# A channel stage in two passes: both block products by Strassen's seven products of 384 columns, with the values between kept in DRAM

## The chip, the cores and the metric

The kernel runs on one core of a Trainium2 chip. The metric is the device time of one execution in microseconds; lower is better. Three executions of the kernel before took 703.06 to 704.03 us, with a median of 703.39 us.

## What is computed

Three blocks follow one another: a windowed and dilated attention over 4 batches, 8 heads and 576 tokens, a gated feed-forward block, and a mixer block. All is single precision. The change touches only the end of the mixer, its channel stage:

```python
h = np.maximum(xt @ w_tok1, 0.0) @ w_tok2        # token stage
u = x + h.transpose(0, 2, 1)
h2 = np.maximum(u @ w_ch1, 0.0) @ w_ch2          # channel stage
return (u + h2).astype(np.float32)
```

Here u has 2304 tokens of 512 channels, w_ch1 is 512 by 1536 and w_ch2 is 1536 by 512.

## The kernel before

**Numbers.** Every operand of a matmul is held as two parts, a high part rounded to the engine's fp32r type and a low part that holds the rest. One product of two blocks is three matmuls (high by high, high by low, low by high), issued by `mm3` (L445). `split` (L461) makes the two parts: a copy on ACT or DVE, then a subtraction on DVE. The weights come from DRAM as 64-bit floats; `single` (L492) turns them into 32-bit ones with one step on ACT and two on DVE.

**Order of the work.** Nothing is issued directly. `Plan` (L148) records every operation with its dependences, prices it (`_cost`, L245), and then `order` (L291) simulates the five engines: each engine takes the ready operation that is due first, where due times are counted back from the matmuls in the order in which the program names them. The result is one fixed order for each engine. All DMAs are issued by SP and share one queue; the plan books a DMA of 32-bit words of n per partition with `8 * (0.03 + 4 * n * 0.0266e-3)` us, at least 0.45, and 2.1 us more until a consumer may start. In the run each engine keeps the planned order, so an instruction that waits holds back all that stand behind it on its engine.

**Channel stage.** The tokens are cut into chunks of 512 (`CH`), four whole ones and one of 256. u lies in SBUF (`whole`, two slots of 4608 words). The loop at L1050 runs over two groups of hidden blocks, five chunks in each, and three values of j in each chunk: 30 steps. For each step `middle` (L997) computes hidden blocks j and j + 6 of the chunk by `w_ch1`: for a whole chunk with Strassen's seven products of 256 columns (each is 2 slices by 3 matmuls, so 42 matmuls), for the last one with four products (24 matmuls). `kept` and `plus` (L980, L985) take sums out of PSUM, `put` (L990) applies the relu and splits. One step later `result` (L1029) multiplies both hidden blocks by `w_ch2` in the plain way: 4 output blocks by 2 by 3, so 24 matmuls of 512 columns (256 in the last chunk). After three steps the sums leave PSUM; those of the first group go to DRAM (`parts`), and come back to be added in the second. `prep_u` (L950) makes Strassen's sums of u and splits them, once for each chunk in each group. `weight_1` (L833) and `weight_2` (L849) load and split the weights; four of each are resident.

Of the kernel before, what the change touches and what calls it, by code (L numbers as in the profile page):

```python
# [54 lines left out]
CH = 512  # L55
# [361 lines left out]
def tile_model(nc, banks, parts, units, cst, mu, w_k, w_v, w_r, w_t1, w_t2, w_c1, w_c2, outT):  # L417
# [5 lines left out]
    def at(place, shape, dtype=F32):  # L423
        name, number, offset = place
        return memory[name][number].view(offset, shape, dtype)
# [387 lines left out]
    both = at(("raw", 0, 0), (2, 4, 128))  # L813
    sums = at(("raw", 0, 1024), (4, 2, 128))
    LO, HI = slice(0, 2), slice(2, 4)
    GROUP, RESIDENT = 3, 4

    def operands(four, two, one):

        four, two, one = pair(four, (4, 2, 128)), pair(two, (4, 128)), pair(one, (2, 128))  # L820
        named = {f"S{i + 1}": tuple(v[:, i] for v in four) for i in range(4)}
        named.update({f"A1{i + 1}": tuple(v[:, 2 * i:2 * i + 2] for v in two) for i in range(2)}, A22=one)
        return four, two, one, named

    w1 = [
        operands(("wk", 0, 0), ("wk", 1, 0), ("wk", 1, 1024)),
        operands(("wk", 2, 0), ("wk", 3, 0), ("wk", 3, 1024)),
        operands(("xt", 2, 0), ("xt", 0, 0), ("xt", 0, 1024)),
        operands(("at", 0, 0), ("wr", 2, 0), ("wr", 3, 0)),
    ]  # L830
    w2 = [pair(p, (C,)) for p in cut("x2", (5, 6, 0, 1, 2, 3), 1024)]

    def weight_1(j):  # L833

        four, two, one, _ = w1[j % RESIDENT]
        for i in range(2):
            single([(everything, col_block(w_c1, j + 6 * i))], at(("raw", 0, 512 * i), (512,)), raw_c)
        a, b = both[:, 0], both[:, 1]
        combine(sums[:, 0], b[:, LO], b[:, HI], ALU.add)
        combine(sums[:, 1], sums[:, 0], a[:, LO], ALU.subtract)  # L840
        combine(sums[:, 2], a[:, LO], b[:, LO], ALU.subtract)
        combine(sums[:, 3], a[:, HI], sums[:, 1], ALU.subtract)
        split(a, *two)
        split(b[:, HI], *one)
        split(sums, *four)

    both_r = ring(("raw", 0, 0), ("raw", 0, 512))

    def weight_2(j):  # L849
        for i in range(2):  # L850
            weight([(everything, words(w_c2)[rows(j + 6 * i), :])], *w2[2 * (j % RESIDENT) + i], raw_c, both_r)
# [13 lines left out]
    for j in range(2):  # L865
        weight_1(j)
# [70 lines left out]
    spare = [("wk", 1, 1536), ("wk", 3, 1536), ("xt", 0, 1536)]  # L937
    first_r = ring(xt512[8:12], ("wr", 3, 512), z512[8:15], cut("at", (2,), 512))
    other_r = ring(z512[:15], ("y", 0, 0))
    mid_r = ring(cut("z", (5,), 512), spare, [("at", 0, 2048), ("at", 0, 2560)])  # L940
    t_r = ring([("unit", i, 0) for i in range(2)])
    part_r = ring(cut("x2", (4,), 256), cut("at", (1,), 256))
    y_r = ring(xt512[8:12])
    xp_r, yp_r, zp_r = psum(0, 1), psum(2), psum(3)
    uhl, mid, op = {}, {}, {}

    def size_of(c):
        return min(CH, NT - CH * c)

    def prep_u(g, c):  # L950
        b1, b2 = (w[:, :, CH * c:CH * c + size_of(c)] for w in whole)
        h = 256
        ops = {"B11": b1[:, :, :h], "B21": b2[:, :, :h]}
        if size_of(c) == CH:
            ops.update(T1=None, T2=None, B22=b2[:, :, h:], T3=None, T4=None)
            order = ["B11", "T1", "B21", "T2", "B22", "T3", "T4"]
        else:
            ops.update(T5=None)
            order = ["B11", "B21", "T5"]
        formed = {  # L960
            "T1": lambda: (b1[:, :, h:], ops["B11"]), "T2": lambda: (ops["B22"], ops["T1"]),
            "T3": lambda: (ops["B22"], b1[:, :, h:]), "T4": lambda: (ops["B21"], ops["T2"]),
            "T5": lambda: (ops["B21"], ops["B11"]),
        }
        for name in order:
            if ops[name] is None:
                x, y = formed[name]()
                ops[name] = t_r.tile(2, h)
                combine(ops[name], x, y, ALU.subtract)
            r = first_r if (g, c) == (0, 0) else other_r  # L970
            hl = r.tile(2, h, dtype=F32R), r.tile(2, h, dtype=F32R)
            split(ops[name], *hl)
            uhl[name] = hl

    def product(out, a, b, first=True, last=True, goes_on=False):
        for k in range(2):
            (ah, al), (bh, bl) = w1[now % RESIDENT][3][a], uhl[b]
            mm3(out, ah[:, k], al[:, k], bh[:, k], bl[:, k], first and k == 0, last and k == 1, goes_on)

    def kept(p):  # L980
        t = part_r.tile(256)
        copy(t, p)
        return t

    def plus(p, t):  # L985
        out = part_r.tile(256)
        combine(out, p, t, ALU.add)
        return out

    def put(m, half, x):  # L990
        h, l = (v[:, half] for v in mid[m])
        nc.scalar.activation(out=h, in_=x, func=AF.Relu)
        nc.vector.scalar_tensor_tensor(out=l, in0=x, scalar=0.0, in1=f(h), op0=ALU.max, op1=ALU.subtract)

    now = 0

    def middle(c, j):  # L997
        nonlocal now
        now = j
        n = size_of(c)  # L1000
        for m in (j, j + 6):
            mid[m] = tuple(mid_r.tile(n, dtype=F32R) for _ in range(2))
        lo, hi = slice(0, 256), slice(256, 512)
        if n < CH:
            x, y = xp_r.tile(256), yp_r.tile(256)
            product(x, "A11", "B11", last=False)
            product(x, "A12", "B21", first=False)
            put(j, lo, x)
            product(y, "S1", "B11", last=False)
            product(y, "A22", "T5", first=False)  # L1010
            put(j + 6, lo, y)
            return
        x, y, z = xp_r.tile(256), yp_r.tile(256), zp_r.tile(256)
        product(x, "A11", "B11")
        s1 = kept(x)
        product(y, "S1", "T1")
        s5 = kept(y)
        product(z, "A12", "B21")
        put(j, lo, plus(z, s1))
        product(x, "S2", "T2", first=False, goes_on=True)  # L1020
        s2 = kept(x)
        product(y, "S4", "B22", first=False, goes_on=True)
        put(j, hi, plus(y, s2))
        product(x, "S3", "T3", first=False, goes_on=True)
        put(j + 6, hi, plus(x, s5))
        product(x, "A22", "T4", first=False, goes_on=True)
        put(j + 6, lo, x)

    def result(g, c, j):  # L1029
        n, start = size_of(c), CH * c  # L1030
        for kt in range(4):
            if j % GROUP == 0:
                op[kt] = bank(4 + kt, (n,))
            for i in range(2):
                w = w2[2 * (j % RESIDENT) + i]
                mm3(
                    op[kt], w[0][:, rows(kt)], w[1][:, rows(kt)], *mid[j + 6 * i],
                    j % GROUP == 0 and i == 0, j % GROUP == GROUP - 1 and i == 1,
                )
            if j % GROUP == GROUP - 1:  # L1040
                y, part = y_r.tile(n), parts[4 * c + kt][:, :n]
                if g == 0:
                    nc.vector.tensor_tensor(out=y, in0=op[kt], in1=whole[kt // 2][:, kt % 2, start:start + n], op=ALU.add)
                    nc.sync.dma_start(out=part, in_=y)
                else:
                    nc.sync.dma_start(out=y, in_=part)
                    nc.vector.tensor_tensor(out=y, in0=op[kt], in1=y, op=ALU.add)
                    nc.sync.dma_start(out=outT[rows(kt), start:start + n], in_=y)

    nchunk = -(-NT // CH)  # L1050
    steps = [(g, c, j) for g in range(2) for c in range(nchunk) for j in range(GROUP * g, GROUP * g + GROUP)]
    for i in range(len(steps) + 1):
        if i < len(steps):
            g, c, j = steps[i]
            if j % GROUP == 0:
                prep_u(g, c)
            if (g, c, j) == (0, 0, 0):
                weight_1(2)
                weight_1(3)
            middle(c, j)  # L1060
        if i:
            before = steps[i - 1]
            if before[:2] == (0, 0):
                weight_2(before[2])
            result(*before)
            if before == (0, 0, 2):
                weight_2(3)
# [84 lines left out]
```

## Time and profile before

| | |
|---|---|
| median of 3 runs | 703.39 us (703.06 to 704.03) |
| the profiled execution, its own time | 704.08 us |
| its span, first to last instruction | 702.3 us |
| around the span | 1.8 us |
| mean granted TensorE clock | 0.995 of full speed |
| busy: PE, DVE, ACT | 687.2, 500.1, 332.1 us |
| DMA | 65.71 MB, 28.1% of the 16 engines' time |

A matmul is shown with its whole passage through the array, so the records of neighbours overlap and busy time overstates the work. The cost of one is read as the distance between starts. The same holds for DVE, where one instruction starts before the record of the last has ended.

### The profile page before, as it was taken

How to read it: one execution, taken by the hardware profiler on the slowest of the kernel's cores; microseconds unless marked ns; L12 is line 12 of the kernel's file. 1: busy time of each engine (PE TensorE's matmuls, PEld its weight loads, DVE VectorE, ACT ScalarE, POOL GpSimd, SP SyncE). 2: the span in 40 equal slices, each digit the busy share in tenths (PEclk: the TensorE clock that was granted, in tenths of full speed). 3: DMA queues.
4: the chain of work that ended last, by engine and by line, in shares of the span. 5: the costliest groups of instructions: out<-in, count | busy, mean ns of one | idle time of the engine just before them, and what ended most of it. 6: DMA issues, size and time to landing. Idle time of an engine off the chain costs nothing.

```text
span 702.3 us, 11861 instructions
## 1 busy us (share of the span) xinstructions
PE 687.2 (98%) x4513; PEld 612.5 (87%) x4513; DVE 500.1 (71%) x1125; ACT 332.1 (47%) x930; POOL 2.1 (0%) x22
## 2 busy tenths in 40 slices
PE   6899999999999999999999999999999999999998
PEld 6678888888888888888789898998998999889888
DVE  5899995695694596673999799674748975656442
ACT  5899873583364474352675364242333542323210
POOL 0000000000000000000000000000000000000000
PEclk9899999999999999999999999999999999999999
DMA  8978332143221001002332221301012323040302
GB/s 327 387 279 297 109 119 70 59 137 112 66 78 55 16 9 53 1 1 71 103 104 97 70 72 56 115 1 61 12 49 70 131 72 105 16 121 1 120 30 91
DMA packets 32935, 65.71 MB, mean 94 GB/s; under 512 B 3056, under 2 KB 11632, under 8 KB 32880
## 3 DMA queue, kind: packets, MB, share of 16 engines
q1 hardware_dynamic: 32880, 64.97, 28.1%
q8 instruction: 35, 0.57, 0.3%
q14 instruction: 20, 0.16, 0.1%
HBM read 55.52 MB, written 9.44 MB: 92 GB/s over the span
## 4 chain that ended last, share of the span: by engine, by line
PE 87%; DVE 5%; DMA 4%; ACT 2%; issue 1%; SPq 0%; DVEq 0%; ACTq 0%
PE bank L403 87%; DVE z L403 2%; ACT z L403 1%; DMA x<-w_k 1%; DMA wr<-units 1%; DVE x L403 1%; DMA wv<-units 1%; DMA xt<-w_t 1%; DVE at L403 1%; DVE xt L403 0%; DVE raw L403 0%; DVE wv L403 0%; ACT x L403 0%; DVE unit L403 0%; ACT at L403 0%
## 5 line engine op out<-in xcount | busy, mean ns | idle before, releaser
L403 PE MATMUL bank<-z,wk 128*128 128x256 f32 (+1 forms) x1276 | 242.8, 311 | 0.3 <-DVE z L403 0.2
L403 PEld LDWEIGHTS bank<-z,wk 128*128 128x128 f32 x1276 | 201.9, 189 | 11.8 <-DVE z L403 0.8
L403 PE MATMUL bank<-wv,z 128*128 128x512 f32 x432 | 129.6, 403 | 1.1 <-DVE z L403 1.1
L403 PEld LDWEIGHTS bank<-wv,z 128*128 128x128 f32 x432 | 77.9, 188 | 13.7 <-DVE z L403 1.9
L403 PE MATMUL bank<-z,x 128*128 128x512 f32 (+1 forms) x300 | 80.8, 371 | 0.0
L403 ACT ACTIVATE z<-bank 128x384 f32<-128x384 f32 (+3 forms) x78 | 36.6, 473 | 74.7 <-PE bank L403 73.9
L403 PE MATMUL bank<-wk,x 128*128 128x512 f32 (+1 forms) x180 | 66.3, 371 | 0.0
L403 PE MATMUL bank<-wr,z 128*128 128x512 f32 x228 | 62.5, 402 | 0.7 <-DVE z L403 0.7
L403 DVE SCALAR_TENSOR_TENSOR z<-bank,z 128x384 f32<-128x384 f32 (+2 forms) x59 | 32.8, 564 | 41.5 <-ACT z L403 41.4
L403 ACT ACTIVATE at<-at 128x96 f32<-128x96 f32 (+3 forms) x155 | 51.1, 332 | 21.8 <-DVE at L403 20.6
L403 ACT ACTIVATE x<-bank 96x512 f32<-96x512 f32 (+2 forms) x68 | 35.1, 519 | 51.5 <-PE bank L403 50.4
L403 PEld LDWEIGHTS bank<-z,x 128*128 128x128 f32 x300 | 52.3, 189 | 7.0
L403 PE MATMUL bank<-at,x 128*128 128x512 f32 (+1 forms) x180 | 53.7, 372 | 0.0
L403 DVE TENSOR_TENSOR z<-z,z 128x384 fp32r<-128x384 f32 x92 | 50.3, 553 | 3.5 <-ACT z L403 1.3
L403 PEld LDWEIGHTS bank<-wr,z 128*128 128x128 f32 x228 | 41.4, 188 | 8.4 <-DVE z L403 1.1
L403 PE MATMUL bank<-z,at 128*128 128x256 f32 (+1 forms) x196 | 46.0, 342 | 0.0
L403 PEld LDWEIGHTS bank<-wk,x 128*128 128x128 f32 x180 | 34.0, 189 | 3.9
L403 PEld LDWEIGHTS bank<-at,x 128*128 128x128 f32 x180 | 32.4, 189 | 4.9
L403 PEld LDWEIGHTS bank<-z,at 128*128 128x128 f32 x196 | 32.4, 190 | 2.7
L403 PE MATMUL bank<-at,z 128*128 128x288 f32 x192 | 33.4, 302 | 1.1 <-DVE wv L403 1.1
L403 DVE SCALAR_TENSOR_TENSOR z<-xt,cst,z 128x256 f32<-128x256 f32 (+3 forms) x92 | 33.7, 404 | 0.6
L403 ACT ACTIVATE z<-z 128x384 fp32r<-128x384 f32 x56 | 28.8, 520 | 8.0 <-DVE z L403 5.9
(163 smaller groups left out, 1071.7 us busy)
## 6 DMA issues: line engine op xcount, KB each, us to landing
wr<-w_c SPq DMA_DIRECT2D x24, 512.0 KB, 3.6
at<-units SPq DMA_DIRECT2D x14, 416.0 KB, 3.5
unit<-units SPq DMA_DIRECT2D x13, 416.0 KB, 3.3
at<-units SPq DMA_DIRECT2D x21, 256.0 KB, 2.9
part<-xt SPq DMA_DIRECT2D x16, 256.0 KB, 2.0
xt<-part SPq DMA_DIRECT2D x16, 256.0 KB, 2.8
outT<-xt SPq DMA_DIRECT2D x16, 256.0 KB, 2.0
wv<-units SPq DMA_DIRECT2D x9, 416.0 KB, 6.9
```

The source lines that it names most:

```text
L403: call(kw["out"], kw["constant"]) if method == "memset" else call(**kw)
```

## The change

Each chunk is now 768 tokens, in two halves of 384 (`N2`), so there are three chunks and no odd one. Pass 1 runs `middle` for three chunks and six j, with all of w_ch1 resident; the relu of the four quarters stays one single-precision block, which goes to DRAM (`kept_mid`). `weight_2` forms Strassen's sums of w_ch2, splits them and stores them to DRAM as well (`kept_w`), through three buffers (`fresh`), and u goes to DRAM too (`kept_u`). Then w_ch2 in its seven forms is read back into the places of w_ch1, and pass 2 runs `result` for the three chunks: each of seven sweeps is 2 output blocks by 6 hidden blocks by 3 matmuls of 384 columns. It reads the hidden values and u back, forms the differences, and splits. The output block leaves once, without `parts`.

```diff
-CH = 512
+N2 = 384
+NAMES = "A11", "S1", "A12", "S2", "S4", "S3", "A22"
...
+    fresh = ring(cut("x2", (4,), 512), ("y", 0, 0))
+    def quarters(j, load, order):
+        for i in range(2):
+            single([(everything, load(j + 6 * i))], at(("raw", 0, 512 * i), (512,)), raw_c)
+        a11, a12, a21, a22 = (both[:, k // 2, k % 2] for k in order)
+        combine(sums[:, 0], a21, a22, ALU.add)
+        combine(sums[:, 1], sums[:, 0], a11, ALU.subtract)
+        combine(sums[:, 2], a11, a21, ALU.subtract)
+        combine(sums[:, 3], a12, sums[:, 1], ALU.subtract)
+        return a11, a12, a22
...
     def weight_2(j):
-        for i in range(2):
-            weight([(everything, words(w_c2)[rows(j + 6 * i), :])], *w2[2 * (j % RESIDENT) + i], raw_c, both_r)
+        a11, a12, a22 = quarters(j, lambda m: words(w_c2)[rows(m), :], (0, 2, 1, 3))
+        for name, v in zip(NAMES, (a11, sums[:, 0], a12, sums[:, 1], sums[:, 3], sums[:, 2], a22)):
+            t = fresh.tile(2, 256, dtype=F32R)
+            split(v, t[:, 0], t[:, 1])
+            nc.sync.dma_start(out=kept_w[name][:, j], in_=f(t))
...
-    for j in range(2):
+    for j in range(3):
         weight_1(j)
...
+    for j in range(3, 6):
+        weight_1(j)
+    mid_r = ring(cut("at", (0,), 4 * N2))
+    x_r, y_r, z_r = psum(0, 1, 2), psum(3, 4, 5), psum(6, 7)
...
+    def prep_u(c):
+        lo, hi = slice(2 * N2 * c, 2 * N2 * c + N2), slice(2 * N2 * c + N2, 2 * N2 * c + 2 * N2)
+        for q in range(2):
+            nc.sync.dma_start(out=kept_u[c][:, 2 * q:2 * q + 2], in_=whole[q][:, :, 2 * N2 * c:2 * N2 * c + 2 * N2])
...
+        for name, x, y in (("S1", b12, "A11"), ("S2", b22, "S1"), ("S3", b22, None), ("A22", b21, "S2")):
+            v[name] = diff_r.tile(2, N2)
...
+            combine(v[name], x, b12 if y is None else v[y], ALU.subtract)
...
     def middle(c, j):
...
+        def part(q, p, t):
+            combine(mid[:, q], p, t, ALU.add)
+            relu(mid[:, q], mid[:, q])
...
+        by(x, "A11")
+        s1 = aside(x)
+        by(y, "S1")
+        s5 = aside(y)
+        by(z, "A12")
+        part(0, z, s1)
+        by(x, "S2", **on)
+        s2 = aside(x)
+        by(y, "S4", **on)
+        part(1, y, s2)
+        by(x, "S3", **on)
+        part(3, x, s5)
+        by(x, "A22", **on)
+        relu(mid[:, 2], x)
+        nc.sync.dma_start(out=kept_mid[c][:, :, j], in_=mid)
+
+    for c in range(3):
+        prep_u(c)
+        for j in range(6):
+            middle(c, j)
+            if c == 0:
+                weight_2(j)
...
+            nc.sync.dma_start(out=f(at(places[j], (n, 2, 256), F32R)), in_=kept_w[name][:, j:j + n])
...
+    def result(c):
+        def load(q):
+            quads[q] = [half_r.tile(3, N2) for _ in range(2)]
+            for i, t in enumerate(quads[q]):
+                nc.sync.dma_start(out=t, in_=kept_mid[c][:, q, 3 * i:3 * i + 3])
+        def parts(q):
+            for t in quads[q]:
+                hl = tuple(hl_r.tile(3, N2, dtype=F32R) for _ in range(2))
+                split(t, *hl)
+        def turned(q, other):
+            for t, o in zip(quads[q], quads[other]):
+                combine(t, o, t, ALU.subtract)
+        def sweep(name, b, banks, **kw):
+            for a in range(2):
+                lhs = [tuple(v[:, rows(a)] for v in hl) for hl in w2[name]]
+                product(banks[a], lhs, b, **kw)
...
+        load(0)
+        load(1)
+        for kt in range(4):
+            nc.sync.dma_start(out=us[kt], in_=kept_u[c][:, kt])
+        load(2)
+        load(3)
+        sweep("A11", parts(0), x)
+        s1 = two(aside_r)
+        plus(x, u_of(0, 0), s1)
+        turned(0, 1)
+        sweep("S1", parts(0), y)
...
+        less(2, 0)
+        sweep("A22", parts(2), x, **on)
+        t = two(out_r)
+        plus(x, u_of(2, 0), t)
+        send(t, 2, 0)
...
-    steps = [(g, c, j) for g in range(2) for c in range(nchunk) for j in range(GROUP * g, GROUP * g + GROUP)]
```

## Rows read from the trace of the kernel before

**Rows 1.** The page: busy time of each engine, and the granted clock in 40 slices.

```profile
PE 687.2 (98%) x4513; PEld 612.5 (87%) x4513; DVE 500.1 (71%) x1125; ACT 332.1 (47%) x930; POOL 2.1 (0%) x22
PEclk9899999999999999999999999999999999999999
```

**Rows 2.** Busy time by stretch: length, engines, then clock, DMA share, GB/s.

```profile
400.00:415.00 15.00, 13.69 (x100) 12.78 (x98) 14.36 (x30) 9.47 (x18) 0.00 (x0) 1.00 0.24 72
415.00:500.00 85.00, 84.93 (x534) 76.73 (x535) 63.48 (x137) 32.59 (x76) 0.00 (x0) 1.00 0.15 50
500.00:600.00 100.00, 100.00 (x665) 92.11 (x665) 68.67 (x148) 35.05 (x78) 0.00 (x0) 1.00 0.24 80
600.00:699.00 99.00, 99.00 (x639) 90.06 (x637) 49.98 (x106) 25.00 (x58) 0.00 (x0) 1.00 0.19 61
```

**Rows 3.** Timeline of PE: start, duration, form and count; unbroken runs of matmuls.

```profile
303.87 2.24 PE L403 MATMUL bank<-wv,z 128*128 128x512 f32 x9
305.95 2.27 PE L403 MATMUL bank<-z,wk 128*128 128x384 f32 x12
308.06 2.24 PE L403 MATMUL bank<-wv,z 128*128 128x512 f32 x9
...
690.42 3.04 PE L403 MATMUL bank<-z,wk 128*128 128x256 f32 x24
...
693.30 0.64 PE L403 MATMUL bank<-z,x 128*128 128x256 f32 x4
```

**Rows 4.** Timeline, the last instructions of the span.

```profile
697.55 2.49 SPq L403 DMA_DIRECT2D outT<-xt  x4
...
698.70 0.52 PE L403 MATMUL bank<-at,x 128*128 128x256 f32 x3
...
699.26 0.42 DVE L403 TENSOR_TENSOR xt<-bank,xt 128x256 f32<-128x256 f32 x1 [0.29 <-PE bank L403]
```

**Rows 5.** Timeline of PE: its two waits where the channel stage begins.

```profile
402.67 1.81 PE L403 MATMUL bank<-at,z 128*128 128x288 f32 x12 [0.51 <-DVE wv L403]
405.07 1.85 PE L403 MATMUL bank<-at,z 128*128 128x288 f32 x12 [0.60 <-DVE wv L403]
```

**Rows 6.** Timeline of DVE: neighbours without a wait, at 384, 256, 512 and 1024 columns.

```profile
304.75 0.56 DVE L403 SCALAR_TENSOR_TENSOR z<-bank,z 128x384 f32<-128x384 f32 x1
305.22 1.28 DVE L403 SCALAR_TENSOR_TENSOR x<-x,bank 128x512 f32<-128x512 f32 x2
...
423.59 0.42 DVE L403 SCALAR_TENSOR_TENSOR at<-bank,at 128x256 fp32r<-128x256 f32 x1
423.93 1.28 DVE L403 TENSOR_TENSOR z<-unit,z 128x512 fp32r<-128x512 f32 x2
425.13 0.69 DVE L403 TENSOR_TENSOR unit<-wv,wv 128x512 f32<-128x512 f32 x1
...
427.90 1.22 DVE L403 TENSOR_TENSOR at<-raw,at 128x1024 fp32r<-128x1024 f32 x1
429.02 0.42 DVE L403 COPY at<-bank 128x256 f32<-128x256 f32 x1
```

**Rows 7.** Groups of ACT's instructions by form: busy, mean ns of one, idle before.

```profile
L403 ACT ACTIVATE z<-bank 128x384 f32<-128x384 f32 x48 | 23.4, 487 | 56.2 <-PE bank L403 55.8
```

**Rows 8.** DMA issues: count, KB each, median us from issue to landing.

```profile
wr<-w_c SPq DMA_DIRECT2D x24, 512.0 KB, 3.6
part<-xt SPq DMA_DIRECT2D x16, 256.0 KB, 2.0
```

**Rows 9.** Stretches in which DMA was busy; the last two columns are DMA share and GB/s.

```profile
8.00:16.00 8.00, 7.59 (x61) 6.95 (x60) 6.79 (x19) 5.43 (x27) 0.00 (x0) 1.00 1.03 401
542.00:545.00 3.00, 3.00 (x27) 3.00 (x26) 0.85 (x2) 0.77 (x2) 0.00 (x0) 1.00 0.83 233
681.00:686.00 5.00, 5.00 (x29) 4.34 (x29) 2.56 (x4) 0.00 (x0) 0.00 (x0) 1.00 0.46 169
```

**Rows 10.** A stretch with DMA and DVE both full: PE is the first busy column.

```profile
48.00:60.00 12.00, 11.26 (x90) 9.89 (x89) 12.00 (x22) 11.81 (x35) 0.00 (x0) 1.00 0.86 314
```

More of the change, by code (lines that the diff above doesn't have):

```diff
@@ L812, in tile_model @@
     raw_c = ring([("wr", k, 0) for k in range(2)])
[L813 to L831, printed above, removed]
-    def weight_1(j):
-        four, two, one, _ = w1[j % RESIDENT]
-        for i in range(2):
[L837 to L845, printed above, removed]
@@ L847, in tile_model @@
-    both_r = ring(("raw", 0, 0), ("raw", 0, 512))
-    def weight_2(j):
-        for i in range(2):
-            weight([(everything, words(w_c2)[rows(j + 6 * i), :])], *w2[2 * (j % RESIDENT) + i], raw_c, both_r)
+    both, sums = at(("raw", 0, 0), (2, 2, 256)), at(("raw", 0, 1024), (4, 256))
+    spots = cut("wk", range(4), 512) + cut("xt", (2, 0), 512) + cut("wr", (2,), 512) + cut("x2", (5, 6, 0, 1, 2, 3), 512)
+    fresh = ring(cut("x2", (4,), 512), ("y", 0, 0))
[8 more added lines that the diff above has]
+        return a11, a12, a22
@@ new lines, in tile_model @@
+    w1 = []
+    def weight_1(j):
+        _, _, a22 = quarters(j, lambda m: col_block(w_c1, m), (0, 1, 2, 3))
+        places = [at(p, (2, 256), F32R) for p in spots[7 * j:7 * j + 7]]
+        for n, part in enumerate((sums[:, 0:2], sums[:, 2:4], both[:, 0])):
+            split(part, *places[2 * n:2 * n + 2])
+        one = places[6][:, 0], places[6][:, 1]
+        split(a22, *one)
+        hl = [tuple(v[:, k] for v in places[2 * n:2 * n + 2]) for n in range(3) for k in range(2)] + [one]
+        names = "S1", "S2", "S3", "S4", "A11", "A12", "A22"
+        w1.append({name: tuple(v.split(2, 128) for v in pair_of) for name, pair_of in zip(names, hl)})
@@ L934, in tile_model @@
     tokens_out(3)
[L937 to L973, printed above, removed]
@@ L975, in product @@
-    def product(out, a, b, first=True, last=True, goes_on=False):
[L976 to L993, printed above, removed]
@@ L995, in tile_model @@
-    now = 0
-    def middle(c, j):
[L998 to L1027, printed above, removed]
@@ L1029, in result @@
-    def result(g, c, j):
-        n, start = size_of(c), CH * c
-        for kt in range(4):
[L1032 to L1048, printed above, removed]
@@ L1050, in tile_model @@
-    nchunk = -(-NT // CH)
-    steps = [(g, c, j) for g in range(2) for c in range(nchunk) for j in range(GROUP * g, GROUP * g + GROUP)]
[L1052 to L1067, printed above, removed]
-            if before[:2] == (0, nchunk - 1) and before[2] < 2:
-                weight_1(before[2] + RESIDENT)
-                weight_2(before[2] + RESIDENT)
+    def product(out, a, b, first=True, last=True, goes_on=False):
+        for k, ((ah, al), (bh, bl)) in enumerate(zip(a, b)):
+            mm3(out, ah, al, bh, bl, first and k == 0, last and k == len(b) - 1, goes_on)
@@ new lines, in tile_model @@
+    for c in range(3):
[4 more added lines that the diff above has]
+                weight_2(j)
+    w2_at = [
+        cut("wk", (0, 1), 512)[:6], cut("wk", (1, 2), 512)[2:], cut("wk", (3,), 512) + cut("x2", (4,), 512),
+        cut("wr", (2,), 512) + cut("x2", (5, 6), 512), cut("x2", (0, 1), 512)[:6],
+        cut("x2", (1, 2, 3), 512)[2:], cut("wr", (0, 1, 3), 512),
+    ]
+    w2 = {}
+    for name, places in zip(NAMES, w2_at):
+        w2[name] = [tuple(at(p, (2, 256), F32R)[:, i] for i in range(2)) for p in places]
+        j = 0
+        while j < 6:
+            n = next(n for n in range(6 - j, 0, -1) if places[j + n - 1][:2] == places[j][:2])
+            nc.sync.dma_start(out=f(at(places[j], (n, 2, 256), F32R)), in_=kept_w[name][:, j:j + n])
+            j += n
@@ new lines, in tile_model @@
+    size = 3 * N2
+    half_r = ring(
+        cut("wv", (0,), size), ("raw", 0, 0), [("z", i, 0) for i in range(6)], ("at", 2, 0), cut("at", (0,), size, 2),
+    )
+    hl_r = ring(cut("wv", (1,), size), cut("xt", (2, 0, 1), size))
+    u_r = ring(("unit", 0, 0), ("unit", 1, 0), ("raw", 0, size), ("at", 0, 2 * size))
+    aside_r = ring(cut("at", (1,), N2), [("z", i, size) for i in range(4)])
+    out_r = ring([("z", 4, size), ("z", 5, size), ("y", 0, 0)])
+    x_r, y_r, z_r = psum(0, 1, 2, 3), psum(4, 5), psum(6, 7)
@@ new lines, in result, with less, plus, send @@
+    def result(c):
+        us = [u_r.tile(2, N2) for _ in range(4)]
+        quads = {}
+        def load(q):
[3 more added lines that the diff above has]
+        def parts(q):
+            out = []
+            for t in quads[q]:
+                hl = tuple(hl_r.tile(3, N2, dtype=F32R) for _ in range(2))
+                split(t, *hl)
+                out += [tuple(v[:, k] for v in hl) for k in range(3)]
+            return out
+        def less(q, other):
+            for t, o in zip(quads[q], quads[other]):
+                combine(t, t, o, ALU.subtract)
+        def turned(q, other):
+            for t, o in zip(quads[q], quads[other]):
+                combine(t, o, t, ALU.subtract)
[3 more added lines that the diff above has]
+                product(banks[a], lhs, b, **kw)
+        def plus(ps, others, tiles):
+            for p, o, t in zip(ps, others, tiles):
+                combine(t, p, o, ALU.add)
+        def send(tiles, kt, half):
+            for a, t in enumerate(tiles):
+                at_t = 2 * N2 * c + N2 * half
+                nc.sync.dma_start(out=outT[rows(kt + a), at_t:at_t + N2], in_=t)
+        def two(r):
+            return [r.tile(N2) for _ in range(2)]
+        def u_of(kt, half):
+            return [us[kt + a][:, half] for a in range(2)]
+        x, y, z = two(x_r), two(y_r), two(z_r)
+        on = dict(first=False, goes_on=True)
+        load(0)
+        load(1)
+        for kt in range(4):
+            nc.sync.dma_start(out=us[kt], in_=kept_u[c][:, kt])
[6 more added lines that the diff above has]
+        sweep("S1", parts(0), y)
+        s5 = two(aside_r)
+        plus(y, u_of(2, 1), s5)
+        sweep("A12", parts(2), z)
+        t = two(out_r)
+        plus(z, s1, t)
+        send(t, 0, 0)
+        turned(0, 3)
+        sweep("S2", parts(0), x, **on)
+        s2 = two(aside_r)
+        plus(x, u_of(0, 1), s2)
+        sweep("S4", parts(3), y, **on)
+        t = two(out_r)
+        plus(y, s2, t)
+        send(t, 0, 1)
+        less(3, 1)
+        sweep("S3", parts(3), x, **on)
+        t = two(out_r)
+        plus(x, s5, t)
+        send(t, 2, 1)
+        less(2, 0)
+        sweep("A22", parts(2), x, **on)
+        t = two(out_r)
+        plus(x, u_of(2, 0), t)
+        send(t, 2, 0)
@@ L1073, in _layout @@
+    for c in range(3):
+        result(c)
 def _layout(a):
@@ L1143, with drawer @@
             banks = [sums.tile([128, 512], F32, name=f"bank{i}", tag=f"bank{i}") for i in range(8)]
-            parts = [dram.tile([128, CH], F32, name=f"part{i}", tag=f"part{i}") for i in range(4 * -(-NT // CH))]
+            def drawer(name, dtype, *shape):
+                return dram.tile([128, *shape], dtype, name=f"part_{name}", tag=f"part_{name}")
+            kept_w = {n: drawer(n, F32, 6, 2, 256) for n in NAMES}
+            kept_u = [drawer(f"u{c}", F32, 4, 2 * N2) for c in range(3)]
+            kept_mid = [drawer(f"mid{c}", F32, 4, 6, N2) for c in range(3)]
             plan = Plan(nc)
-            tile_model(plan, banks, parts, *aps, out)
+            tile_model(plan, banks, kept_w, kept_u, kept_mid, *aps, out)
             with tc.manual_schedule():
```

30 lines of the change are left out of this document (29 added, 1 removed).

## The prediction, made before the changed kernel ran

> **What bounds the kernel now.** I read the page first: PE is busy for 687.2 of 702.3 us and its clock is granted almost in full throughout [rows 1]. Then the stretches: from 415 us to the last matmul PE hardly stops, while DVE is busy for 69% between 500 and 600 us and 50% after that, and DMA for 15 to 24% [rows 2]. So in the stage that changes, time is the number of matmuls times their distance, and everything else is cover. A busy share cannot price a matmul, since records overlap, so I read distances of starts [rows 3]: nine of 512 columns take 2.08 us, 231 ns each; twelve of 384 take 2.11 us, 175.8 ns; 24 of 256 take 2.88 us, 120.0 ns. The ends around the stage: two waits of 0.51 and 0.60 us for DVE at its start [rows 5], and behind the last matmul one eviction of 0.42 us and a store [rows 4]. The profiled execution took 704.1 us; the median is 0.7 lower, which I take off at the end.
>
> **Columns.** Before, 24 steps of whole chunks have 42 matmuls of 256 columns and 24 of 512 each; the 6 steps of the short chunk have 24 + 24 of 256. That is 24 x 42 + 6 x 48 = 1296 of 256 and 576 of 512: 1296 x 0.1200 + 576 x 0.2311 = 155.5 + 133.1 = 288.6 us. After, each pass has 3 chunks x 6 blocks x 42 = 756 matmuls of 384 columns, 1512 in all: 1512 x 0.1758 = 265.8 us, 132.9 for each pass. **The difference is 22.8 us**, and it lies wholly on the path. The Trainium skill, "TensorE: Matmul & The Clock Gate", section "Back-to-back issue gap", gives a warm gap of N / 2.4 + 2.5 ns; by it this term would be 20.1 us, an estimate, since all three distances here are longer than it says (231 against 216 at 512 columns).
>
> **DVE and ACT.** DVE starts its next instruction 0.34 us after one of 256 columns, 0.47 after 384, 0.60 after 512 and 1.12 after 1024 [rows 6]; on that line 768 cost 0.86 and 1152 cost 1.25. Pass 1: eleven steps of 768 for the sums of u in each chunk, 9.5 us; three additions of 384 for each block, 18 x 3 x 0.47 = 25.4; each weight step has four integer steps at 512, at most 2.4 us, four sums, 1.4, and seven low parts, 2.4 (2.1 in `weight_1`, where they are joined): 6 x 6.2 + 3 x 5.9 = 54.9. In all 28.5 + 25.4 + 54.9 = 109 of 132.9 us, 82%. Pass 2, each chunk: 14 low parts and 8 differences of 1152, 27.5 us, and 14 additions of 384, 6.6: 34.1 of 44.3 us, 77%. So DVE is hidden on average but with less room than the 69% it had. The relus can go to ACT: seven steps of 384 for each block at 0.49 us [rows 7] are 3.4 us beside 7.4 us of PE.
>
> **DMA.** Bytes in pass 1: values between 18 x 786 KB = 14.2 MB, forms of w_ch2 42 x 262 KB = 11.0, u 4.7, raw weights 18 x 524 KB = 9.4; in all 39.3 MB. Scaled to a full share, DMA moved 281 GB/s (weights in short runs), 367 (stores and reloads of 2 KB runs) and 389 (attention units) [rows 9]. The pass would need 101 to 140 us of its 132.9. The nearest row is that of 2 KB runs, so I expect 107 to 120 us: nearly full, not over. Pass 2 moves 34.6 MB, 89 to 123 us. Read latency is covered, as the places for the next operands are free steps ahead: the first form of w_ch2 takes the place of w_ch1's block 0, dead five blocks (37 us) before the pass ends.
>
> **Where PE can wait,** each bounded from both sides. (a) Start: the sums of u for a first chunk are 11 x 0.86 = 9.5 us of DVE, before 11 x 0.60 = 6.6, against a first block of 7.4 us, before 5.0. Between 0 and +2.9 us; I take +0.5, by the two small waits there now. (b) End: an eviction and store of 384 instead of 256 columns, +0.1 each. (c) Between the passes, 0 to 6 us: a 512 KB load lands in 3.6 us [rows 8], and a first form three times as large, if late, cannot cost much more. I take 0, because three sets of banks and early free places cover it. (d) Stores: the plan books a block of values (786 KB) at 1.55 us of queue; at 389 to 281 GB/s it is 2.0 to 2.8, so what stands behind it is 0.5 to 1.25 us late, mean 0.86. A DVE step that waits for a `fresh` buffer holds back the evictions behind it, which PE needs within about one product (1.05 us). For the 12 blocks of the first two chunks, a third of 0.86 each: 3.4 us, from bounds of 0 and the 25 us of the second rival. The sum: 704.1 - 22.8 + 0.5 + 0.2 + 3.4 = 685.4, less 0.7: **685 us**.
>
> **Rivals.** First, **DMA bounds pass 1**. Besides the 39.3 MB, about 6 MB of operands for pass 2 should be read before the pass ends: 45 MB at 310 GB/s are 145 us, 12 more than PE needs: 704.1 - 22.8 + 0.7 + 12 - 0.7 = 693. For it: where DMA and DVE were both full, PE was busy for only 11.26 of 12 us [rows 10], and most stores come in runs of 1.5 and 2 KB. Against: spread over both passes it is 74 MB in 266 us, and no reader waits for most of it.
>
> Second, the one on the other side: **the ring of three buffers stops DVE or ACT**. Each of the 42 stores of w_ch2's forms needs a free `fresh` buffer; the split that waits for it holds the in-order queue, with the evictions of `middle` behind. At 0.6 us of PE each, the size of the waits that PE has for DVE now [rows 5], that is 25 us: 681.3 + 25.2 = 706.5. It decides from 22.1 / 42 = 0.53 us for each store on. For it: the planned order cannot move when stores queue behind blocks of values. Against: a 256 KB store lands in 2.0 us [rows 8] where the plan books 0.68 + 2.1 = 2.8 for it, and the forms have a whole pass to be made. The Trainium skill, "DMA: Bandwidth & Descriptors", section "Anatomy of one DMA", says that a DMA's fixed 2 us are mostly the wait for the write's receipt, surprisingly long for HBM. [...]
>
> Third, **the handover inside a block**: S3 and A22 add into the same bank with nothing of the same block between, and no second product's matmuls are left to fill in. If the next block's first product isn't put there, 18 x 0.6 us [rows 5] = 11 us: 692. Against: three banks for that sum, and the plan takes any ready matmul.
>
> **How the numbers follow.** 0.2%, 1.4 us, is about what a measurement of this kernel can tell from no change. Forecast 0.58 (679.5 to 688), DMA bound 0.15 (688 to 702), handover 0.10 (689 to 698), the ring 0.14 (over 705), a mixture that just balances 0.03. Faster is 0.58 + 0.15 + 0.10 = 0.83, less 0.01 for the first rival's upper end; slower is 0.14, no change 0.04. The range runs from 679.5, the columns with no wait at all and a little for their distance, to 701: it leaves out the ring and about 0.05 of the others' ends.
>
> **What would show it.** In the profile after, 1512 matmuls of 384 columns at about 176 ns in unbroken runs; pass 1 about 133 to 138 us long with DMA at 75 to 95%, pass 2 at 133 to 135 with DMA at 60 to 80%; PE's waits for DVE and ACT below 5 us in sum. If the first rival holds, PE, ACT and DVE wait for SP's stores in pass 1 in long pieces. If the second holds, DVE or ACT waits on the tiles x and y of the ring, many times and briefly, with PE waiting behind. If the third holds, there are 18 even gaps, one in each block. The prediction is wrong if runs of 384 columns have another distance, or if pass 2, which has no stores on its path, also has PE idle for more than 3 us.

## The result, and the profile after

The changed kernel takes 679.03 us (678.60 to 679.83) against 703.40 us: a ratio of 0.9654, 95% interval 0.9637 to 0.9671. On two other chips it took 679.68 and 679.97 us, with ratios of 0.9666 and 0.967. The prediction said 685 us, 679.5 to 701: the direction and the cause were right, the gain of 24.4 us was a third larger than the 18.4 forecast, and the time lies half a microsecond under the range. On the two other chips, beside 702.06 and 703.19 us for the kernel before, the gain was 22.4 and 23.2 us.

The page of the changed kernel: busy time by engine, then clock and DMA in 40 slices, as in [rows 1].

```profile
PE 662.2 (98%) x4153; PEld 611.3 (90%) x4153; DVE 541.1 (80%) x1082; ACT 340.8 (50%) x895; POOL 2.1 (0%) x22
...
PEclk9999999999999999999999999999999999999999
DMA  8988332234322001100434259977889999532211
```

PE has 360 matmuls fewer; DVE is fuller, and DMA, busy for 15 to 24% of this stage before [rows 2], is now at 70% or more from slice 25 to slice 34. By stretches of the two passes (columns as in [rows 2]):

```profile
407.00:542.00 135.00, 134.27 (x775) 132.72 (x774) 115.22 (x225) 70.27 (x140) 0.00 (x0) 1.00 0.91 333
543.00:674.00 131.00, 131.00 (x756) 130.71 (x755) 110.10 (x117) 26.80 (x24) 0.00 (x0) 1.00 0.47 168
```

Pass 2 is 756 matmuls in 131.0 us without any idle time: 173.3 ns for each. Pass 1 with DMA at 0.91 and 333 GB/s is what the prediction expected of it, and DVE at 85% is near its 82. Pass 2 is not: it is shorter than the 133 to 135 us expected, DMA is at 0.47 instead of 0.60 to 0.80 (168 GB/s for 131 us are 22 MB, not 34.6, so part of its operands came earlier), and DVE at 84% instead of 77. The timeline of PE, as [rows 3], shows the distance in long runs, and the older one in the same kernel's earlier stage:

```profile
304.79 2.27 PE L404 MATMUL bank<-z,wk 128*128 128x384 f32 x12
306.90 2.24 PE L404 MATMUL bank<-wv,z 128*128 128x512 f32 x9
...
542.83 6.40 PE L404 MATMUL bank<-wv,wk 128*128 128x384 f32 x36
549.07 7.96 PE L404 MATMUL bank<-xt,wk 128*128 128x384 f32 x45
556.87 0.68 PE L404 MATMUL bank<-wv,wk 128*128 128x384 f32 x3
```

From 304.79 to 306.90 are 2.11 us for twelve, 175.8 ns each, as before. From 542.83 to 549.07 are 6.24 us for 36, and from 549.07 to 556.87 are 7.80 for 45: both 173.3. With the 120.0 ns of 256 columns [rows 3] the line, for N columns, is 13.3 ns + N / 2.4 GHz. The run that the prediction read stands behind one of 512 columns and carries 0.03 us of that change of form (experiment 7).

PE's waits from the token stage to pass 2 (all of them, from the timeline, answering to [rows 5]) and the waits of DVE and ACT for the new stores, in the same stretch (us in total, times, longest):

```profile
400.99 1.81 PE L404 MATMUL bank<-at,z 128*128 128x288 f32 x12 [0.51 <-DVE wv L404]
404.85 1.84 PE L404 MATMUL bank<-at,z 128*128 128x288 f32 x12 [2.05 <-DVE wv L404]
...
439.59 2.03 PE L404 MATMUL bank<-z,x 128*128 128x384 f32 x10 [0.15 <-DVE at L404]
...
451.84 2.01 PE L404 MATMUL bank<-z,x 128*128 128x384 f32 x10 [0.50 <-ACT at L404]
```

```profile
ACT x L404 <- DMA part_A<-x: 6.2, 4, 2.5
ACT x L404 <- DMA part_S<-x: 3.4, 3, 2.9
ACT y L404 <- DMA part_S<-y: 2.9, 2, 1.9
...
DVE y L404 <- DMA part_S<-y: 2.0, 1, 2.0
DVE x L404 <- DMA part_S<-x: 1.3, 1, 1.3
```

So the second rival's waits are there, 15.8 us of them on the two engines, and PE idles for only 0.65 us once pass 1 runs. Its wait of 2.05 us comes before that, and from the same cause: ACT waits for a buffer of the ring, DVE's half of the split waits for ACT, and the eviction `wv<-bank` that PE needs stands behind that.

```profile
402.60 0.42 ACT L404 ACTIVATE x<-raw 128x256 fp32r<-128x256 f32 x1 [2.48 <-DMA part_A<-x]
```

```profile
403.05 0.43 DVE L404 TENSOR_TENSOR x<-raw,x 128x256 fp32r<-128x256 f32 x1 [1.51 <-ACT x L404]
...
404.34 0.82 DVE L404 TENSOR_TENSOR wv<-bank,wv 128x288 f32<-128x288 f32 x2
```

The stores of forms, of 256 KB each, are slower than the 2.8 us that the plan books for them (median from issue to landing; before, one of that size took 2.0 us, [rows 8]):

```profile
part_mid<-at SPq DMA_DIRECT2D x18, 768.0 KB, 5.1
...
part_S<-x SPq DMA_DIRECT2D x16, 256.0 KB, 4.3
part_A<-x SPq DMA_DIRECT2D x12, 256.0 KB, 4.4
```

The end of the span answers to [rows 4]: the eviction takes 0.56 instead of 0.42 us.

```profile
674.07 0.56 DVE L404 TENSOR_TENSOR y<-bank,at 128x384 f32<-128x384 f32 x1 [2.57 <-PE bank L404]
```

### The profile page after: what moved, and what is told of

It reads as the page before. It is cut to its first block, busy times and chain, and to the rows that moved or that the text cites. A ratio compares the mean times of both kernels' runs of the same rounds, so it can differ in the third digit from the quotient of the medians.

```text
span 677.5 us, 11254 instructions
## 1 busy us (share of the span) xinstructions
PE 662.2 (98%) x4153; PEld 611.3 (90%) x4153; DVE 541.1 (80%) x1082; ACT 340.8 (50%) x895; POOL 2.1 (0%) x22
## 4 chain that ended last, share of the span: by engine, by line
PE 74%; DVE 15%; DMA 5%; ACT 4%; issue 2%; SPq 0%; DVEq 0%; ACTq 0%
PE bank L404 74%; DVE raw L404 4%; DVE z L404 3%; DVE x L404 2%; DMA part_S<-x 2%; DVE wv L404 2%; DMA part_S<-y 1%; DVE at L404 1%; ACT z L404 1%; ACT at L404 1%; ACT x L404 1%; DMA wr<-w_c 1%; DMA raw<-w_v 1%; DVE unit L404 1%; DVE xt L404 1%
## 5 line engine op out<-in xcount | busy, mean ns | idle before, releaser
L404 PE MATMUL bank<-z,wk 128*128 128x384 f32 x774 | 175.9, 343 | 0.2
L404 PEld LDWEIGHTS bank<-z,wk 128*128 128x128 f32 x774 | 136.7, 188 | 7.6 <-DVE z L404 1.1
L404 ACT ACTIVATE at<-at 128x96 f32<-128x96 f32 (+2 forms) x181 | 64.9, 362 | 36.4 <-DVE at L404 35.3
L404 PE MATMUL bank<-xt,wk 128*128 128x384 f32 x266 | 57.5, 345 | 0.0
L404 DVE TENSOR_TENSOR z<-z,z 128x384 fp32r<-128x384 f32 (+1 forms) x94 | 53.1, 571 | 3.5 <-ACT z L404 1.3
L404 PE MATMUL bank<-xt,x 128*128 128x384 f32 x256 | 51.8, 334 | 0.0
L404 PEld LDWEIGHTS bank<-xt,wk 128*128 128x128 f32 x266 | 46.7, 188 | 1.2
L404 DVE TENSOR_TENSOR at<-bank,at 128x384 f32<-128x384 f32 x64 | 35.3, 554 | 14.7 <-PE bank L404 13.1
L404 PEld LDWEIGHTS bank<-xt,x 128*128 128x128 f32 x256 | 45.0, 188 | 0.0
L404 PE MATMUL bank<-z,x 128*128 128x384 f32 x206 | 43.8, 336 | 0.7 <-ACT at L404 0.5
```

The costliest lines, as they stand in the source:

```text
L404: call(kw["out"], kw["constant"]) if method == "memset" else call(**kw)
```

## The experiments

Theory: the stage costs its matmuls at 13.3 ns + N / 2.4, and waits of DVE and ACT are kept from PE by the planned order. Rivals: the distance is 175.8 ns and something else was won; PE's lead in PSUM banks hides the waits; the stores do cost PE several microseconds.

**1. The second product in the plain way.**

```diff
-        for name, v in zip(NAMES, (a11, sums[:, 0], a12, sums[:, 1], sums[:, 3], sums[:, 2], a22)):
+        for name, v in zip(PLAIN, (both[:, 0, 0], both[:, 1, 0], both[:, 0, 1], both[:, 1, 1])):
...
+            p, q = parts(half), parts(2 + half)
+                sweep(PLAIN[2 * pair_of], p, banks_of, last=False)
+                sweep(PLAIN[2 * pair_of + 1], q, banks_of, first=False)
```

> The second product goes back to the plain way, eight sweeps a chunk instead of seven, all else as in the changed kernel: 864 matmuls of 384 columns in pass 2 instead of 756. Theory 'columns at 173.3 ns' (the stage costs matmuls times 13.3 ns + N / 2.4, whatever the other engines do): 108 x 0.1733 = 18.7 us more, 697.7 us, and pass 2 lasts 149.7 us without idle PE. Theory 'columns at 175.8 ns, and some 3 to 6 us won elsewhere by the change' (fewer operations of DVE, no partial sums through DRAM): the distance in runs is 175.8, or the time is below 696, since pass 2 loses its eight differences of 1152 columns a chunk and pass 1 stores 24 forms instead of 42.

Measured: 699.26 us (698.48 to 700.04), ratio 0.9952 (0.9939 to 0.9965). Pass 2, from its first matmul on, in the stretches view:

```profile
544.24:693.90 149.66, 149.66 (x865) 149.60 (x864) 47.21 (x55) 11.04 (x10) 0.00 (x0) 1.00 0.34 116
```

864 matmuls at 173.3 ns would be 149.7 us; PE never idles, though DVE fell from 110 to 47 us. So Strassen in the second product is worth the 18.7 us of its columns and nothing that DVE does there counts. The time is 1.6 us over the first theory's 697.7. Against 679.7, from another chip, the whole is 19.6; the rest is within what else the plan shifted, such as a new wait of 2.7 us in pass 1:

```profile
434.36 1.41 PE L405 MATMUL bank<-z,xt 128*128 128x384 f32 x4 [2.70 <-DVE wr L405]
```

**2. Every store of a form issued twice.**

```diff
             nc.sync.dma_start(out=kept_w[name][:, j], in_=f(t))
+            nc.sync.dma_start(out=again_w[:, (7 * j + NAMES.index(name)) % 8], in_=f(t))
```

> Each of the 42 stores of a form of w_ch2 is issued a second time to a place that nothing reads: 11 MB more in pass 1. Theory 'PE has lead enough, DMA is the next bound': pass 1 moved 332 GB/s x 133 us = 44 MB at a share of 0.91; with 55 MB at 332 / 0.91 = 365 GB/s it needs 151 us, so PE idles up to 18 us there, less what can be read later: 684 to 697 us. Theory 'queue waits don't reach PE at all': below 681 us. Theory of the second rival (each store that waits costs PE 0.5 us or more): 42 more stores, 700 us or more.

Measured: 696.01 us (694.26 to 696.73), ratio 0.9896 (0.9866 to 0.9926), at the upper end of what the first theory gives. The largest part of the loss is one wait between the passes, 6.13 us of PE, and the stretch around it shows a granted clock of 0.82; nine shorter waits in pass 1 make 6.2 us more. Ahead of the long one DVE stood at a load of hidden values:

```profile
545.00:564.00 19.00, 12.87 (x64) 12.55 (x64) 9.18 (x12) 3.66 (x6) 0.00 (x0) 0.82 0.99 368
```

```profile
556.00 1.36 DVE L404 TENSOR_TENSOR wv<-z,wv 128x1152 f32<-128x1152 f32 x1 [6.20 <-DMA z<-part_mid]
557.27 0.55 DVE L404 TENSOR_TENSOR at<-bank,at 128x384 f32<-128x384 f32 x1
```

The second line is an eviction of pass 1, queued behind a subtraction of pass 2. DMA was busy for 0.95 of pass 1, and ACT and DVE waited 27.8 us for buffers that the second stores still held. So 11 MB more do reach PE. How much of the 16 us is DMA's rate, and how much the held buffers and a load that the plan booked too short (experiments 5 and 6), this run does not separate.

**3. Five banks instead of eight in pass 1.**

```diff
-    x_r, y_r, z_r = psum(0, 1, 2), psum(3, 4, 5), psum(6, 7)
+    x_r, y_r, z_r = psum(0, 1), psum(3, 4), psum(6)
```

> Pass 1 uses five PSUM banks (2, 2, 1) instead of eight (3, 3, 2) for its three sums; nothing else changes. Theory 'the banks give PE its lead over DVE and ACT, and the lead swallows their waits for the stores': PE idles 5 to 15 us more in pass 1, 684 to 694 us, in many short waits. Theory 'the waits fall where PE needs nothing from DVE and ACT': within 1.5 us of the changed kernel, 677.5 to 680.5.

Measured: 681.83 us (680.35 to 683.36), ratio 0.9703 (0.9675 to 0.973). Both ranges were missed, the first by more: after its start, pass 1 has three waits of PE of 0.31, 0.89 and 0.35 us instead of 0.65 in all. Even that is within what executions differ by: the repeats of the changed kernel (experiment 8) have 0.27 and 1.67 us. So the lead that the three banks gave is not what swallows the waits; what the five left still hide was not tried.

**4. The stores' time taken out of the plan.**

```diff
+            nc.quick.add(i)
+            nc.ops[i] = {e: (m, kw, 0.05) for e, (m, kw, _) in nc.ops[i].items()}
...
-                    ready[s][o] = max(ready[s][o], end + self.TAIL[e] + self.DELAY[e][o])
+                    ready[s][o] = max(ready[s][o], end + (0.0 if i in self.quick else self.TAIL[e] + self.DELAY[e][o]))
```

> The plan books nothing for the 42 stores of forms (0.05 us, and no delay until the buffer is free again); the instructions are the same, only their order on the engines can differ. Theory 'the waits for the three buffers cost PE little because the plan books 2.8 us for each and puts other evictions ahead': now splits stand in the queues 2 to 4 us too early, DVE and ACT wait 2 to 3 times as long as the 16 us there now, PE idles 8 to 25 us: 687 to 704 us. Theory 'PE is far enough ahead of DVE and ACT for such waits whatever the plan books': below 682 us.

Measured: 702.10 us (699.65 to 704.60), ratio 0.9988 (0.9968 to 1.0008): **the whole gain is gone**, with the same computation and the same bytes. DVE and ACT now wait twice as long for stores of forms, 33.9 us instead of 15.8 (the largest groups are shown; for all other transfers they wait 1.8 us), and PE behind them:

```profile
ACT x L405 <- DMA part_S<-x: 13.3, 9, 4.7
ACT x L405 <- DMA part_A<-x: 10.5, 3, 5.2
DVE y L405 <- DMA part_A<-y: 4.0, 1, 4.0
```

```profile
404.64 3.22 PE L405 MATMUL bank<-at,z 128*128 128x288 f32 x12 [4.98 <-DVE wv L405]
...
441.40 1.65 PE L405 MATMUL bank<-z,xt 128*128 128x384 f32 x4 [3.66 <-ACT wr L405]
...
487.66 1.31 PE L405 MATMUL bank<-z,wk 128*128 128x384 f32 x6 [3.03 <-DVE at L405]
```

Ahead of the second of these waits ACT's queue shows how: the eviction `wr<-bank` stands behind splits that wait for the ring.

```profile
437.77 0.42 ACT L405 ACTIVATE x<-raw 128x256 fp32r<-128x256 f32 x1 [3.31 <-DMA part_A<-x]
...
440.88 0.47 ACT L405 ACTIVATE wr<-bank 128x384 f32<-128x384 f32 x1
```

PE's waits sum to 17.4 us where the changed kernel has 3.2, and its mean clock over pass 1 is 0.96. This is the second rival's mechanism: 22.4 us beside the changed kernel on the same chip, where the rival was priced at 25. It does not decide in the changed kernel, because the plan books 2.8 us for each store, and the order that it makes with that keeps most of the waits from PE.

**5. Forms of w_ch2 no earlier than pass 1.**

```diff
+                if j == 0:
+                    for i in range(first, len(nc.ops)):
+                        nc.deps[i].add(behind)
```

> The plan may begin with the forms of w_ch2 only after the first eviction of pass 1, instead of in the token stage. Theory 'PE's wait of 2.05 us where pass 1 begins is the second rival's mechanism: ACT waited 2.48 us for a buffer of the ring, DVE behind it, and the eviction that PE needed behind DVE': that wait falls back to about 0.6, no wait for stores before pass 1, 1 to 1.5 us faster than the changed kernel. Theory 'DVE is simply full there': the wait stays near 2 us, and the time within 0.5 us.

Measured: 692.12 us (691.15 to 693.44), ratio 0.9848 (0.9826 to 0.9871). The wait at the start went as the first theory says, and yet the kernel is 12.4 us slower: the forms that were begun early are missing later. One wait between the passes is half of it; eight shorter ones in pass 1 make 4.8 us more.

```profile
403.61 1.85 PE L404 MATMUL bank<-at,z 128*128 128x288 f32 x12 [0.42 <-DVE wv L404]
...
554.38 2.29 PE L404 MATMUL bank<-z,x 128*128 128x384 f32 x6 [6.16 <-DVE at L404]
```

```profile
552.49 1.36 DVE L404 TENSOR_TENSOR wv<-z,wv 128x1152 f32<-128x1152 f32 x1 [5.86 <-DMA z<-part_mid]
```

It is the wait of experiment 2: a load for pass 2, planned too short, holds DVE while pass 1 still has evictions.

**6. The new DRAM transfers at their measured price,** first alone, then with experiment 5's edit.

```diff
+            if any(not isinstance(kw[k], View) and Plan._kept(kw[k]) for k in ("out", "in_")):
+                return 512 * cols / 330e3
             return max(0.45, 8 * (0.03 + 4 * cols * 0.0266e-3))
```

> The plan prices every DMA to and from the new DRAM places at 330 GB/s (768 KB 2.4 us instead of 1.55, 256 KB 0.79 instead of 0.68). Theory 'DVE and ACT wait because blocks of values take longer than booked': their waits for stores fall from 16 us to below 8, the time changes by less than 1 us, since PE idles only 0.65 us behind the start. Theory 'what is left of PE's idle time comes from these waits, the start included': 1 to 3 us faster.

> The changed kernel with the new DRAM transfers priced at 330 GB/s in the plan, once more, beside the changed kernel. Theory 'DVE's and ACT's waits behind the stores cost PE next to nothing once they are planned': 0 to 1 us faster than the changed kernel of this call. Theory 'they cost what PE idles after the start': 1 to 3 us faster.

Measured: 678.06 us (677.77 to 679.50) beside 679.68 for the changed kernel on one chip, 680.10 (677.24 to 680.43) beside 679.97 on another: no difference that these times can tell. The profiles can: from the start of the matmuls behind the wait of 0.51 us to the end of the span, the two take 274.7 and 274.1 us, the changed kernel 276.5 to 277.4 (experiment 8). The waits for stores of forms fell from 15.8 to 4.3 us and PE has no wait left in pass 1, so by the stage the 15.8 were worth some 2 to 3 us, as the second theory says, and not nothing. The first of the two profiles begins the stage at 401.3 us, the second at 404.4, and such differences hide the gain in the times.

```profile
ACT x L406 <- DMA part_A<-x: 2.5, 2, 1.9
...
DVE x L406 <- DMA part_A<-x: 1.0, 1, 1.0
ACT x L406 <- DMA part_S<-x: 0.8, 2, 0.5
```

> Both edits of the plan: forms of w_ch2 only after the first eviction of pass 1, and the new DRAM transfers priced at 330 GB/s. Theory 'the 12 us that the later forms cost came from transfers that the plan priced too low, so that DVE stood 5.9 us at a load of hidden values with evictions of pass 1 behind it': with the right price that wait goes, 677 to 680 us, PE's wait at the start below 0.6. Theory 'later forms leave DMA too little time before pass 2, whatever the plan knows': 686 us or more, with the wait between the passes again.

Measured: **676.19 us** (675.54 to 677.34), ratio 0.9622 (0.9606 to 0.9638), beside 679.97 and 0.967 (0.9654 to 0.9685) for the changed kernel on that chip. It is the fastest version here, by 3.8 us, and the two intervals do not meet; the first theory's 677 to 680 us was missed by 0.8. PE's only waits are the two at the start, 0.93 us; pass 1 has none:

```profile
401.12 1.82 PE L406 MATMUL bank<-at,z 128*128 128x288 f32 x12 [0.51 <-DVE wv L406]
403.37 1.85 PE L406 MATMUL bank<-at,z 128*128 128x288 f32 x12 [0.42 <-DVE wv L406]
...
539.42 6.40 PE L406 MATMUL bank<-wv,wk 128*128 128x384 f32 x36
```

```profile
407.00:542.00 135.00, 135.00 (x784) 134.77 (x783) 122.23 (x240) 74.10 (x151) 0.00 (x0) 1.00 0.91 319
```

From 401.12 to the start of pass 2 at 539.42 are 138.3 us; in the changed kernel, from 400.99 to 542.83, 141.8. These 3.5 us are nearly the whole gain. They lie at the waits: 1.6 us are the wait at the start, 0.65 the waits in pass 1 (in the chain of work that ended last, stores of forms stand ahead of them at 425.6, 430.7 and 443.5 us), and 1.3 lie in 20 matmuls of pass 1, most of that beside the waits, which the next one follows after 0.18 to 0.41 us instead of 0.173. Here the waits cost more than their idle time.

**7. Matmuls of 192 columns in half of pass 2.** The two halves of a bank begin their sums separately, which changes what these blocks sum; number, order and form of the matmuls are as told.

```diff
+                        for cs in (slice(0, 192), slice(192, 384)):
+                            nc.tensor.matmul(
+                                out=banks[a][:, cs], lhsT=l, rhs=r[:, cs], start=first and k == 0 and n == 0,
```

> In pass 2 the matmuls of every second output block are cut into two of 192 columns: 378 matmuls of 384 become 756 of 192, the columns stay the same. Theory 'a matmul costs 13.3 ns + N / 2.4 wherever its neighbours have its own form': 93.3 ns for each of 192, 378 x 13.3 = 5.0 us more, 684.5 us; where a run of one form is followed by the other, the run looks 20 to 40 ns too long, which is what made 384 columns look like 175.8 ns in the run of twelve that the prediction used. Theory 'a matmul costs its columns, and 384 were faster in pass 2 for another reason, such as quiet DMA or other operands': no more than 1 us, and the 384 beside the 192 stay at 173.3 with nothing between runs. Theory 'the load of the weights sets the least distance': 118 ns or more for each of 192, 378 x 63 = 24 us.

Measured: 699.72 us (698.02 to 700.15), ratio 0.9951 (0.9933 to 0.9968). The timeline of PE, 384 and 192 columns in turn:

```profile
637.50 1.76 PE L404 MATMUL bank<-wv,wr 128*128 128x384 f32 x9
639.10 1.72 PE L404 MATMUL bank<-xt,wr 128*128 128x384 f32 x9
640.66 2.15 PE L404 MATMUL bank<-wv,wr 128*128 128x192 f32 x18
642.64 2.17 PE L404 MATMUL bank<-xt,wr 128*128 128x192 f32 x18
644.65 5.53 PE L404 MATMUL bank<-xt,wk 128*128 128x384 f32 x38
```

The first nine of 384 stand behind a run of 192 and take 1.60 us; the second nine stand behind their own form and take 1.56, 173.3 ns each, although 192 columns follow. So a change of form adds 0.04 us, and to the run behind it, not to the one ahead as I had expected. An earlier stage of the kernel before shows the same between 512 and 384 columns:

```profile
310.14 2.27 PE L403 MATMUL bank<-z,wk 128*128 128x384 f32 x12
312.24 2.92 PE L403 MATMUL bank<-wr,z 128*128 128x512 f32 x12
315.00 2.20 PE L403 MATMUL bank<-wv,z 128*128 128x512 f32 x9
317.04 2.27 PE L403 MATMUL bank<-z,wk 128*128 128x384 f32 x12
```

Twelve of 512 behind 384 take 2.76 us, 230.0 ns each; nine behind those take 2.04, 226.7 each, which is 13.3 + 512 / 2.4. The 192 take 1.98 and 2.01 us for 18, 110 to 112 ns each, where 13.3 + 80 would be 93.3 and the weight theory asked for 118. The first theory's edges were found, its 684.5 us was not, and the other two theories missed as well. 756 x 111.7 - 378 x 173.3 = 18.9 us accounts for the 19.7 lost. Below some width the distance no longer follows the columns; 256 at 120.0 ns is still on the line. The Trainium skill, "TensorE: Matmul & The Clock Gate", section "LDWEIGHTS (loading the stationary operand)", puts the load of a weight of P columns at P / 1.2 ns; for 128 that makes 107 ns, an estimate, which is near that floor. In the trace the records of loads last 188 ns or more and overlap, so they show no load by itself, and that the load causes the floor was not tried.

**8. The kernel before with three blocks of w_ch1 ready ahead of the token stage, and the changed kernel repeated.**

```diff
-    for j in range(2):
+    for j in range(3):
         weight_1(j)
```

> The kernel before, with the third block of w_ch1 prepared ahead of the token stage as in the changed kernel, and nothing else of the change. In the two profiles the channel stage begins 1.7 us earlier in the changed kernel. Theory 'that comes from this move or from the other order that it gives the first stages': 701 to 702.5 us. Theory 'it is a matter of the profiled executions, or of work the move only shifts': 703 to 704 us.

> The changed kernel once more, beside the others of this call on one chip, so that they can be compared with it. Every theory: 678 to 680 us, ratio to before 0.964 to 0.967; unbroken runs of 384 columns in pass 2 at 173.3 ns. Theory 'the channel stage began 1.7 us earlier because of the clock in the profiled execution of before, which fell between 20 and 40 us': the start of the stage differs between executions by 1 to 2 us while the length of the stage, 275.5 to 277 us from that start to the end of the span, does not.

> The changed kernel, to stand beside the other three of this call on their chip. Every theory: ratio to before 0.964 to 0.968, 678 to 681 us.

Measured: 702.83 us beside 702.63, ratio 1.0003 (0.9989 to 1.0017); that move is worth nothing that the runs can tell. The repeats of the changed kernel are those above. In the profiles, from the start of the matmuls behind the 0.51 us wait to the end of the span, the kernel before takes 702.3 - 402.67 = 299.6 us and this variant 701.7 - 402.09 = 299.6; the changed kernel takes 276.5, 277.4 and 277.1. The stage therefore gains 22.2 to 23.1 us, and the start of the stage, between 401.0 and 402.7 us, differs by execution. The first profile of the kernel before had a granted clock of 0.79 and 0.87 between 20 and 40 us, the changed kernel's had 1.00, and its stage began 1.7 us earlier. That the clock did this is not shown: this variant's profile had 1.00 there as well and began the stage at 402.09, that of experiment 6's last run 0.85 and 0.97 and began it at 401.12.

## Why the prediction was right and where it was wrong

**What bounds the kernel, and what the change saves: right.** Time went with the number and form of matmuls, DVE at 85% of pass 1 stayed cover, and experiment 1 shows each matmul of 384 columns at its price.

**Columns: right in kind, the term 1512 x 0.1758 was mis-sized.** Measured it is 1512 x 0.1733 = 262.1 instead of 265.8: 3.7 us, the largest part of the miss. I took the distance from one run of twelve, whose beginning held 0.03 us for the change from 512 columns; the changed stage has one form only. The run of 256 stood behind its own form and had no such edge. The 231.1 ns of 512 columns had one too, but there it belonged: in the stage before, 256 and 512 take turns, and by their starts the 576 of 512 took 231.7 ns each and all 1872 matmuls 288.8 us, against 288.6 in the prediction. By its own sign, "runs of 384 columns have another distance", the prediction was wrong here. The Trainium skill's gap of N / 2.4 + 2.5 ns ("TensorE: Matmul & The Clock Gate", section "Back-to-back issue gap"), which the page gives for an isolated matmul, would have made it 245.7 us, an estimate; the trace has 13.3 in place of 2.5.

**Step (d), 3.4 us for stores: the size was near by luck, the place wrong.** The premise held, stores late by more than booked (4.3 us to land) and DVE and ACT waiting 15.8 us. But the prediction spread the price over the 12 blocks of the first two chunks, and assumed that a late eviction hurts after one product. In pass 1 PE paid at two places, 0.65 us of idle time and 1.3 beside it; another 1.6 it paid at the start, which (d) did not have in view. Together that is the 3.5 us of experiment 6. Experiment 4 shows what holds the rest back: the order, made with each store's round trip in mind. Experiment 3 shows that the last three banks do not.

**Step (a), the start: right place, low.** I took +0.5; the two waits grew from 1.1 to 2.6 us, +1.5. The reason is not the wider sums of u alone: forms are begun in the token stage, and a buffer of the ring held ACT for 2.48 us, DVE behind it. Experiment 5 and the last run of 6 bring the wait back to 0.42. **Step (b)** was 0.2 and measured 0.4 (from the last matmul to the end of the span, 3.6 us instead of 3.2). **Step (c)**, nothing between the passes, held. Experiments 2 and 5 have waits of 6.13 and 6.16 us there, at its bound of 6, but by another path: not a late form of w_ch2, for which the bound was made, but a load of hidden values that DVE waits for with evictions of pass 1 behind it. The agreement is chance.

Together, for the stage in the two profiles: the columns saved 26.7 us (288.8 - 262.1) instead of 22.8; (a) and (d) cost 3.2 (waits behind the first one 2.7 instead of 0.8, and the 1.3) instead of 3.9; (b) 0.4 instead of 0.2. That is 23.1 instead of 18.7, and 23.1 is what the stage gained. So 4.4 of the 6.0 us of the miss are the stage's, nearly all of it the columns. The other 1.6 lie ahead of the stage, which began 1.7 us earlier in one profile than in the other; they differ by execution and chip. With the gains of the two other chips, 22.4 and 23.2 us, 703.4 would have become 681.0 and 680.2, inside the range: that the range was left is in part chance, that the term was too large is not. The range's lower end left 1.1 us for a shorter distance (680.6 with no wait at all), where 3.7 were needed.

**Rivals.** DMA did not bound pass 1 but came close (0.91): it did move the rival's 45 MB there (333 GB/s for 135 us), but at 366 GB/s of a full share, as the 2 KB runs of [rows 9], and not at 310. The ring cost about 3.5 us and would have decided, had the plan not known of it. The handover inside a block did not show: no 18 even gaps.

## What to carry to other kernels

Read a matmul's distance from the longest runs of one form, and from several, before it is multiplied by 1500: 2.5 ns were worth as much as all the waits that the stores caused. A wait that an engine has in its queue costs the critical engine little if the fixed order was made with its length in mind, and much if not: with the same computation and bytes PE waited for 0.9 us with measured prices and later forms, 3.2 in the changed kernel and 17.4 with nothing booked. Price a wait by the stage's length, not by the idle time alone, and compare the stage from its own start, since what comes before it differs by a microsecond or two. When a change fills DMA, price its transfers in the plan by their measured rate, and look for loads of the next phase standing in front of the last evictions of this one.

## What was not expected of the hardware

One matmul of 192 columns takes 110 to 112 ns, hardly less than one of 256 (120.0), in streams where each has its own weights, while 256, 384 and 512 lie on 13.3 ns + N / 2.4 in their cleanest runs (120.0, 173.3, 226.7). A store of 256 KB landed in 2.0 us with DMA at 0.15 to 0.24 of its time and in 4.3 with DMA at 0.91. A change of form added 0.02 to 0.04 us to the run behind it (384 behind 512, 512 behind 384, 384 behind 192); only 192 behind 384 came out 0.03 shorter. What in the engine does this, and what sets the floor near 111 ns, stays open.
